# Attention on one Trainium2 core: joining the score products and the value products of two key chunks

## The chip, the cores and the metric

The kernel runs on one core of one Trainium2 chip. The metric is the device time of one execution in microseconds (us). The kernel before takes 992.52 us, the median of three runs (991.43 to 992.89).

## The reference

Attention with a sigmoid in place of the softmax, then a layer of eight experts with a skip gate, then a dense layer. The change lies in the attention alone.

```python
# q, k, v: (4, 12, 448, 64), float32
scale = 1.0 / np.sqrt(q.shape[-1])
scores = scale * np.matmul(q, k.transpose(0, 1, 3, 2)) - np.log(S)
attn = 1.0 / (1.0 + np.exp(-scores))
attn_out = np.matmul(attn, v)
x = attn_out.transpose(0, 2, 1, 3).reshape(B * S, H * D)      # 1792 x 768
...
# experts: tokens with x @ w_skip > 0 go through one of 8 experts and are added back
# dense layer: h = x @ w_in (768 -> 2048), elu(h) @ w_out (2048 -> 768)
```

## The kernel before, in words

The work has three stages, one after the other: attention (with the routing of the tokens behind it), experts, dense layer. In each of them the order of the instructions on TensorE, VectorE and ScalarE is the order in which the program is written (`manual_schedule`); the order on the DMA queues is set by a planner.

**Steps.** Attention runs over pairs of heads: 4 batches of 6 pairs are 24 steps, n = 0 to 23 (loop at line 448), and a 25th pass, n = 24, that only finishes the last pair. Two steps share a tile T of q and k (four heads); p is the step's place in its tile, hp its place in its batch. In a step the 448 keys are cut into four chunks of 112, c = 0 to 3 (line 479).

**One chunk.** `scores` (line 235) computes, for both heads of the pair, the transposed scores of one chunk: 112 keys by 448 queries. k is split into two float32r parts, kh and kl, and the parts of q lie stacked in qs, so that a head takes two MATMULs (line 239, out<-in `ps<-qs,kh` and `ps<-qs,kl`), four per chunk. Their output is a buffer `ps` of two PSUM banks; there are two such buffers in turn. ScalarE then takes the sigmoid of the whole buffer into the tile `at` (line 246). `mix` (line 250) multiplies a chunk of `at` by the values: for each head one float32 product with 64 output rows, the two heads side by side on the array (line 253, `po<-at,vt`). The trace shows a float32 product as two MATMULs, so a chunk has four of them, in two passes of two heads. The four chunks of a step accumulate in one PSUM bank `po`; behind the last of them VectorE copies it to `xT` (line 261).

**What follows what.** `at` has two buffers, so step n computes the scores of pair n and the value products of pair n - 1: the chunk loop issues scores of chunk c (pair n), then the value products of chunk c (pair n - 1).

**What else is in the chunk loop.** Behind chunks 1 and 3 come the splits of the next tile: ScalarE casts (line 227 for q, line 232 for k), VectorE subtracts (line 228 writes qs, line 233 writes kl). In the steps with p = 0 q is split, in those with p = 1 k. In nine steps a row tile of x is transposed by three plus three small MATMULs (line 138, `px`), copied out by VectorE behind chunk 1 and by ScalarE behind chunk 3 (line 283), and written to HBM. In the second step of batches 1 to 3 the gate logits of the batch before are computed behind chunk 0 (line 267) and copied by VectorE (line 275), and transposed behind chunk 2 (line 138, `pl`). Behind each chunk VectorE does up to two of the six operations that turn a float64 weight into float32 (`narrow`, lines 146 to 166; 18 weights in all, one per step at most, so six operations behind chunks 0, 1 and 2). In the last steps the routing of the first tokens is added (`soon`).

**After attention.** The last logits, the remaining row tiles and the routing follow; the routing yields the experts' numbers, by which the expert weights are fetched (line 693), and the tokens of each block (line 700).

The lines that matter here:

```python
for c in range(NCH):
    if n < steps:
        scores(at, c, p, *cur[1])
    if n:
        mix(c, n - 1, *prev, po)
    if nxt and n < steps and c % 2:
        (split_q, split_k)[p](c // 2, *nxt)
```

Of the kernel before, what the change touches and what calls it, by code (L numbers as in the profile page):

```python
# [32 lines left out]
E = 8  # L33
# [28 lines left out]


def _constants():
    """Identity, triangles and index ramps: they depend on shapes alone."""
    parts = {
        "ident": np.eye(P),
        "fold": np.arange(P)[:, None] % FEW == np.arange(P),
        "tri": np.triu(np.ones((P, P)), 1),
        "iota_r": np.tile(np.arange(P), (P, 1)),  # L70
        "iota_a": np.tile(np.arange(NHB) * P, (P, 1)),
        "rev": np.tile(E - np.arange(E), (P, 1)),
        "row": np.arange(P)[:, None],
        "ramp": np.tile(np.concatenate([np.arange(E), -np.arange(E)]), (P, 1)),
        "per_tok": GATE_UNIT / (np.arange(NTT)[None, :] * P + np.arange(P)[:, None] - NT),
        "tok": np.arange(NTT)[None, :] * P + np.arange(P)[:, None] - NT,
    }
    at = 0
    for name, a in parts.items():
        _CONST_COLS[name] = (at, a.shape[1])  # L80
        at += a.shape[1]
    return np.ascontiguousarray(np.concatenate(list(parts.values()), 1).astype(np.float32))
# [6 lines left out]
def build(nc, tc, a):  # L89
# [3 lines left out]
    with ExitStack() as top:  # L93
# [47 lines left out]
            nc.sync.dma_start(w, wide[i].rearrange("p (n t) -> p n t", t=2)[:, part])  # L141

        def narrow(dst, w, sg, mg, on_act):
            """Two words of a float64 to float32: sign, exponent - 896, top 23 bits."""
            lo, hi = w[:, :, 0], w[:, :, 1]
            nc.vector.tensor_scalar(sg, hi, NEG, None, op0=ALU.bitwise_and)
            yield
            if on_act:
                nc.scalar.activation(dst, hi.bitcast(F32), AF.Abs)
                nc.vector.tensor_scalar(dst, dst, LEAST, MOST, op0=ALU.max, op1=ALU.min)  # L150
            else:
                nc.vector.tensor_scalar(mg, hi, 2**31 - 1, None, op0=ALU.bitwise_and)
                yield
                nc.vector.tensor_scalar(
                    dst, mg.bitcast(F32), LEAST, MOST, op0=ALU.max, op1=ALU.min
                )
            yield
            nc.vector.scalar_tensor_tensor(
                sg, lo, 29, sg, op0=ALU.logical_shift_right, op1=ALU.bitwise_or
            )  # L160
            yield
            nc.vector.tensor_scalar(
                mg, dst.bitcast(I32), 4, NEG, op0=ALU.logical_shift_left, op1=ALU.bitwise_xor
            )
            yield
            nc.vector.scalar_tensor_tensor(
                dst.bitcast(I32), mg, 1, sg, op0=ALU.logical_shift_right, op1=ALU.bitwise_or
            )

# [1 line left out]
        ET = mybir.EngineType  # L171
        with ExitStack() as st:
            st.enter_context(tc.manual_schedule(engines={ET.PE, ET.Activation, ET.DVE}))
# [15 lines left out]
            nc.gpsimd.memset(zero_b, 0.0)  # L189

            def keep_warm(n):
                """Products of zeros that hold TensorE's clock up while it waits."""
                ps = pss.tile([P, 4, P], F32, name="idle", tag="ps")
                for _ in range(n):
                    nc.tensor.matmul(
                        ps, zero_b[:, 0], zero_b.to_broadcast([P, 4, P]), start=True, stop=True
                    )
# [124 lines left out]
            rt_tok = ert([NTT, P], "rt_tok", F16)  # L322

            def choices(a, z):
                """The experts of the tokens of tiles a to z; E stands for none."""
                w, sh = slice(a, z), [P, z - a, E]
                nc.gpsimd.tensor_scalar(oh1[:, w, E], lgt[:, w, E], 0.0, None, op0=ALU.is_le)
                nc.vector.reduce_max(mx[:, w, 0], lgt[:, w, :E], axis=AX.X)
                yield
                nc.vector.tensor_sub(dl[:, w], lgt[:, w, :E], mx[:, w].to_broadcast(sh))  # L330
                yield
                nc.vector.tensor_scalar(
                    skip[:, w], lgt[:, w, E], 0.0, float(NHB * P), op0=ALU.is_le, op1=ALU.mult
                )
                yield
                nc.vector.scalar_tensor_tensor(
                    sc[:, w], dl[:, w], 0.0, grid("rev", z - a, E), op0=ALU.is_ge, op1=ALU.mult
                )
                yield
                nc.vector.reduce_max(m2[:, w, 0], sc[:, w], axis=AX.X)  # L340
                yield
                nc.vector.tensor_add(m2[:, w, 0], m2[:, w, 0], skip[:, w])
                yield
                nc.vector.tensor_tensor(
                    oh[:, w], sc[:, w], m2[:, w].to_broadcast(sh), op=ALU.is_equal
                )
                yield
                with nc.allow_low_precision("whole numbers up to 14"):
                    nc.vector.reduce_sum(
                        per[a > 0][:, 0], oh1[:, w].rearrange("p t e -> p e t"), axis=AX.X  # L350
                    )
# [2 lines left out]
                run(choices(a, z))  # L354

            def positions(a, z, pool, tag):
                """How many tokens before each one have the same expert."""
                pos = pool.tile([P, z - a, E1], F32, name="pos", tag=tag)
                n, w = z - a, oh1[:, a:z]
                if a:  # L360
# [15 lines left out]
                return pos  # L376

            def places(a, z, pos):
                """The tokens' places in their half blocks."""
                w = slice(a, z)  # L380
                nc.vector.tensor_mul(t1[:, w], pos, oh1[:, w])
                yield
                nc.vector.reduce_sum(posv[:, w], t1[:, w], axis=AX.X)
                yield
                nc.vector.tensor_copy(pos_i[:, w], posv[:, w])
                yield
                nc.vector.tensor_scalar(sr_i[:, w, 0], pos_i[:, w], P - 1, None, op0=ALU.bitwise_and)
                yield
                nc.vector.tensor_copy(sr[:, w], sr_i[:, w])
                yield  # L390

            def spots(a, z):
                """One-hot rows of the tokens' places in their half blocks, times the tokens."""
                for t in range(a, z):
                    nc.vector.tensor_scalar(
                        rt_tok[:, t, :], iota_h, sr[:, t, :], con("tok")[:, t : t + 1],
                        op0=ALU.is_equal, op1=ALU.mult,
                    )
                    yield

            def sooner():
                """Routing of the first tiles."""
                yield from choices(0, SOON)
                for _ in range(NCH):
                    yield
# [42 lines left out]
            for n in range(steps + 1):  # L448
# [28 lines left out]
                    row = rows(done_rows, (nc.vector.tensor_copy, nc.scalar.copy))  # L477
                    done_rows += 1
                for c in range(NCH):
                    if n < steps:  # L480
                        scores(at, c, p, *cur[1])
                    if n:
                        mix(c, n - 1, *prev, po)
                    if nxt and n < steps and c % 2:
                        (split_q, split_k)[p](c // 2, *nxt)
                    if row is not None and c in (1, 3):
# [33 lines left out]
            for t in range(done_rows + 1, done_rows + 3):  # L520
                run(rows(t, tail_rows))

# [1 line left out]
            choose(SOON, NTT)  # L524
            cnt = ps1.tile([P, E], F32, name="cnt", tag="po")
            for k_, p in enumerate(per):
# [28 lines left out]
            nc.vector.reduce_sum(bs[:, 0, :], tmp, axis=AX.X)  # L555

            def halves():
                """One-hot columns of the tokens' half blocks."""
                fo = rt([NTT, E], "fo")
                nc.vector.tensor_mul(fo, bs.to_broadcast(sh), oh)  # L560
                yield
# [15 lines left out]
                    aa, sa.to_broadcast([P, NTT, NHB]), grid("iota_a", NTT, NHB), op=ALU.is_equal  # L577
                )

            # block b's expert, on partition b, and how many blocks there are  # L580
            own = rt([2, E], "own")
            nc.vector.tensor_add(span[:, 1], span[:, 0], nb[:, 0])
            nc.vector.scalar_tensor_tensor(
# [25 lines left out]
            nc.vector.tensor_scalar(used, inv, 0.0, None, op0=ALU.is_lt)  # L609
            nc.vector.tensor_copy(slot_off[:, :NHB], inv)  # L610

            # gates of the slots
            ex = rt([NTT, E], "ex")
            nc.scalar.activation(ex, dl, AF.Exp)
            sm = rt([NTT], "sm")
# [29 lines left out]
            nc.vector.tensor_copy(ct[:, 0], ordered)  # L645
            nc.vector.tensor_copy(tok[:, :, 0], con("tok")[:, :NOR])
            nc.vector.tensor_copy(iota_a[:, 0], con("iota_a")[:, :NOR])
# [1 line left out]
        kept = top.enter_context(ExitStack())  # L649
        with ExitStack() as st:  # L650
            st.enter_context(tc.manual_schedule(engines={ET.PE, ET.Activation, ET.DVE}))
# [113 lines left out]
                    )  # L765

            def product(o, h, n, a2, i, c, width, k0, total):
                """One chunk's part of a product whose stationary side is the tokens' columns."""
                t = slice(h * P, (h + 1) * P)
                for j in range(WCH // width):  # L770
                    w = slice(j * width, (j + 1) * width)
# [115 lines left out]
                        )  # L887

            def places_in_order():
                """Skipped tokens come first in the dense layer's order, then the blocks' tokens."""  # L890
                at = 0

                def part(*shape, dt=F32):
# [48 lines left out]
                    )  # L942

            def slot_order():
                """The dense layer's order, its first four columns behind the last block's."""
                og = acc_t[1][:, :NOR]
                for t in range(NOR):
                    nc.tensor.matmul(
# [13 lines left out]
                nc.vector.tensor_scalar_add(order, order_off, float(NT))  # L962

            def close(i):
                """With i blocks in all: the columns of the dense layer's first tokens."""
                if i == 0:
                    run(places_in_order())
                    order_rows()
# [45 lines left out]
            n = nc.values_load(n_blocks[:1, :1], min_val=0, max_val=NB)  # L1014
            level(0, n)

# [1 line left out]
        with ExitStack() as st:  # L1018
            st.enter_context(tc.manual_schedule(engines={ET.PE, ET.Activation, ET.DVE}))
            wsp = st.enter_context(tc.tile_pool(name="wsp", reuse_waits="tile", bufs=2))  # L1020
# [78 lines left out]
                return gh, gl  # L1099

            def regions(acc, t):
                """Where 128 tokens' 768 outputs lie: a bank, and half of one that two share."""
                yield acc[t], slice(0, 512), True
                half = acc[TB + t // 2]
                o = 256 * (t % 2)
# [137 lines left out]
```

## Time and profile before

| | |
|---|---|
| time, median of 3 runs (lowest, highest) | 992.52 us (991.43, 992.89) |
| span of the profiled execution, first to last instruction | 988.9 us |
| own time of the profiled execution | not recorded beside the span; the three runs lie 2.5 to 4.0 us above it |
| TensorE busy | 938.1 us, 95% of the span |
| VectorE, ScalarE busy | 590.0 us, 513.9 us |
| attention, first value product to last | 15.3 to 204.2 us |
| mean granted TensorE clock | 0.977 of full speed |

How to read it: a MATMUL's recorded end is modelled and matmuls overlap in the pipeline, so the busy share of TensorE tells little about how fast it goes. What counts is the distance from the start of one MATMUL to the start of the next. In the views below a row gives the start, the duration, engine, line, operation, the tensors (out<-in) and how many instructions were merged into it.

### The profile page before, as it was taken

The page shows a single profiled execution, that of the slowest core. Times are in us where ns is not written, and L with a number is a line of the kernel's source. Part 1 is how long each engine was busy: PE and PEld are TensorE (multiplying, and loading weights), DVE is VectorE, ACT ScalarE, POOL GpSimd, SP SyncE. Part 2 cuts the span into 40 slices and gives each one's busy share as a digit, 9 for nine tenths or more (in the row PEclk, how much of TensorE's full clock was granted, in tenths as well). Part 3 has the DMA queues.
Part 4 walks back from the last instruction along what each step waited for, and adds up shares of the span by engine and source line. Part 5 has one row for each costly group of instructions (what it writes and reads, how often), then busy time and mean ns, then how long its engine had stood idle before and what let it go on. Part 6 is the DMA issues. An engine that isn't in the chain of part 4 may idle for free. (4 is left out here: it accounts for less than half of the span.)

```text
span 988.9 us, 13865 instructions
## 1 busy us (share of the span) xinstructions
PE 938.1 (95%) x5310; PEld 745.3 (75%) x5310; DVE 590.0 (60%) x890; ACT 513.9 (52%) x700; POOL 60.2 (6%) x66
## 2 busy tenths in 40 slices
PE   8999999988896997978989999999999999999997
PEld 3444444448795897867879999988888888888997
DVE  4776777866743465448868888743444433443664
ACT  7767676634342543447745455444444434444664
POOL 0000000020111010011110000010000000000100
PEclk9999999998998999979999999999999999999999
DMA  9877877449955546558156334110001000000100
GB/s 247 264 228 233 278 219 236 163 166 379 410 185 189 183 158 254 180 205 316 47 210 227 97 96 120 57 65 1 17 17 32 29 37 1 1 1 1 65 1 33
DMA packets 33755, 139.56 MB, mean 141 GB/s; under 512 B 4634, under 2 KB 5274, under 8 KB 33650
## 3 DMA queue, kind: packets, MB, share of 16 engines
q1 hardware_dynamic: 29410, 119.17, 35.9%
q0 software_dynamic: 4240, 19.01, 5.3%
q8 instruction: 63, 1.03, 0.4%
q14 instruction: 42, 0.34, 0.1%
HBM read 117.58 MB, written 22.42 MB: 142 GB/s over the span
## 5 line engine op out<-in xcount | busy, mean ns | idle before, releaser
L719 DVE TENSOR_TENSOR wlo<-raw,whi 128x1536 fp32r<-128x1536 f32 x66 | 115.1, 1758 | 67.5 <-ACT whi L717 65.7
L246 ACT ACTIVATE at<-ps,bias 112x896 f32<-112x896 f32 x96 | 96.7, 1008 | 52.0 <-PE ps L239 50.1
L1094 DVE SCALAR_TENSOR_TENSOR m<-m,acc 128x512 f32<-128x512 f32 (+1 forms) x64 | 39.7, 621 | 140.6 <-ACT m L1093 140.6
L717 ACT CAST whi<-raw 128x1536 fp32r<-128x1536 f32 x66 | 96.5, 1478 | 52.1 <-PE acc L778 23.5
L1092 ACT ACTIVATE m<-acc 128x512 f32<-128x512 f32 (+1 forms) x64 | 34.9, 545 | 168.5 <-PE acc L1085 168.4
L1083 PE MATMUL acc<-x,wih 128*128 128x256 f32 (+1 forms) x360 | 121.5, 338 | 0.0
L1085 PE MATMUL acc<-x,wil 128*128 128x256 f32 (+1 forms) x360 | 121.5, 337 | 0.0
L1084 PE MATMUL acc<-x,wih 128*128 128x256 f32 (+1 forms) x360 | 121.3, 337 | 0.0
L1116 PE MATMUL acc<-wol,gh 128*128 128x256 f32 x320 | 101.1, 316 | 0.0
L1116 PE MATMUL acc<-woh,gl 128*128 128x256 f32 x320 | 100.6, 314 | 0.0
L1116 PE MATMUL acc<-woh,gh 128*128 128x256 f32 x320 | 100.4, 314 | 0.0
L253 PE MATMUL po<-at,vt 112*64 112x448 f32 x384 | 92.5, 563 | 0.0
L239 PE MATMUL ps<-qs,kh 128*112 128x448 f32 x192 | 79.5, 414 | 2.5 <-ACT kh L232 1.9
L239 PEld LDWEIGHTS ps<-qs,kh 128*112 128x112 f32 x192 | 33.9, 177 | 56.0 <-issue 39.5
L1073 DVE TENSOR_TENSOR wol<-wo,woh 128x768 fp32r<-128x768 f32 x64 | 61.2, 957 | 23.3 <-ACT woh L1072 22.9
L1085 PEld LDWEIGHTS acc<-x,wil 128*128 128x128 f32 x360 | 68.0, 189 | 7.7
L1083 PEld LDWEIGHTS acc<-x,wih 128*128 128x128 f32 x360 | 68.1, 189 | 6.4
L1084 PEld LDWEIGHTS acc<-x,wih 128*128 128x128 f32 x360 | 68.1, 189 | 6.3
L239 PE MATMUL ps<-qs,kl 128*112 128x448 f32 x192 | 71.5, 372 | 0.7 <-DVE kl L233 0.7
L1116 PEld LDWEIGHTS acc<-woh,gh 128*128 128x128 f32 x320 | 60.3, 189 | 10.1
L1116 PEld LDWEIGHTS acc<-wol,gh 128*128 128x128 f32 x320 | 60.3, 188 | 9.1
L1072 ACT CAST woh<-wo 128x768 fp32r<-128x768 f32 x64 | 53.3, 833 | 25.9 <-PE acc L1116 25.8
(236 smaller groups left out, 2036.1 us busy)
## 6 DMA issues: line engine op xcount, KB each, us to landing
raw<-in_w SPq DMA_DIRECT2D x66, 768.0 KB, 6.1
kr<-in_k SPq DMA_DIRECT2D x22, 448.0 KB, 6.3
raw<-in_wi SPq DMA_DIRECT2D x9, 768.0 KB, 7.8
raw<-in_wo SPq DMA_DIRECT2D x9, 768.0 KB, 7.2
vt<-in_v SPq DMA_DIRECT2D x12, 448.0 KB, 5.1
x_d<-xr SPq DMA_DIRECT2D x14, 384.0 KB, 2.7
raw<-in_wi SPq DMA_DIRECT2D x14, 384.0 KB, 3.0
raw<-in_wo SPq DMA_DIRECT2D x14, 384.0 KB, 3.0
```

Source lines behind the costliest of these rows:

```text
L239: nc.tensor.matmul(ps[:CP, j, :S], kk[:, 2 * p + j, c * CP : (c + 1) * CP], qs[:, p, j], start=(i == 0), stop=(i == 1),)
L246: nc.scalar.activation(at[:, :, c, :], ps[:CP, :, :S], AF.Sigmoid, bias=bias[:CP], scale=QK_SCALE)
L253: nc.tensor.matmul(po[64 * j : 64 * j + 64, :S], vt[:, 2 * (hp % 2) + j, c, :], at[:, j, c, :], start=(c == 0), stop=(c == NCH - 1),)
L717: nc.scalar.copy(w_hi, raw)
L719: nc.vector.tensor_sub(w_lo, raw, w_hi)
L1072: nc.scalar.copy(pair[0], wo_r[f])
L1073: nc.vector.tensor_sub(pair[1], wo_r[f], pair[0])
L1083: nc.tensor.matmul(o, a, b, start=(cc == 0), stop=False)
L1084: nc.tensor.matmul(o, a, c, start=False, stop=False)
L1085: nc.tensor.matmul(o, wil[:, cc], b, start=False, stop=(cc == KD - 1))
L1094: nc.vector.scalar_tensor_tensor(m[:, :n], m[:, :n], -1.0, ph[:, :n], op0=ALU.add, op1=ALU.max)
L1116: nc.tensor.matmul(o, a, b, start=(clears and f == 0 and k_ == 0), stop=(f == KF2 - 1 and k_ == 2), skip_group_check=True,)
```

## The change

The chunk loop issues the scores of two chunks, c and c + 1, and then the value products of the same two chunks of the preceding pair, each time c is even. At odd c it issues neither. Everything else in the loop stays where it was: splits, row tiles, logits, weight conversion and routing. The rest of the difference between the two files removes comments.

```diff
                 for c in range(NCH):
-                    if n < steps:
-                        scores(at, c, p, *cur[1])
-                    if n:
-                        mix(c, n - 1, *prev, po)
+                    if c % 2 == 0:
+                        for c2 in (c, c + 1):
+                            if n < steps:
+                                scores(at, c2, p, *cur[1])
+                        for c2 in (c, c + 1):
+                            if n:
+                                mix(c2, n - 1, *prev, po)
                     if nxt and n < steps and c % 2:
                         (split_q, split_k)[p](c // 2, *nxt)
```

TensorE, the first half of a step with neither logits nor a row tile (two chunks), before. `x2` stands for the two value products of a chunk:

```order
L239 MATMUL ps<-qs,kh 112x448
L239 MATMUL ps<-qs,kl 112x448
L239 MATMUL ps<-qs,kh 112x448
L239 MATMUL ps<-qs,kl 112x448
L253 MATMUL po<-at,vt 64x448 x2
L239 MATMUL ps<-qs,kh 112x448
L239 MATMUL ps<-qs,kl 112x448
L239 MATMUL ps<-qs,kh 112x448
L239 MATMUL ps<-qs,kl 112x448
L253 MATMUL po<-at,vt 64x448 x2
```

And now:

```order
L239 MATMUL ps<-qs,kh 112x448
L239 MATMUL ps<-qs,kl 112x448
L239 MATMUL ps<-qs,kh 112x448
L239 MATMUL ps<-qs,kl 112x448
L239 MATMUL ps<-qs,kh 112x448
L239 MATMUL ps<-qs,kl 112x448
L239 MATMUL ps<-qs,kh 112x448
L239 MATMUL ps<-qs,kl 112x448
L253 MATMUL po<-at,vt 64x448 x4
```

The same instructions stand in two runs in place of four, so TensorE goes from scores to value products and back once per two chunks in place of twice.

VectorE, one step (n = 8) from its conversion's first operation to the next step's, before (`sg`, `mg`, `mf` are the conversion, `qs` the split of q, `xr` a row tile, `xT` the copy of the finished pair):

```order
L146 TENSOR_SCALAR sg<-raw_106 128x768
L152 TENSOR_SCALAR mg<-raw_106 128x768
L228 TENSOR_TENSOR qs<-qr,qs 64x896
L283 COPY xr<-px 128x384
L154 TENSOR_SCALAR mf<-mg 128x768
L158 SCALAR_TENSOR_TENSOR sg<-raw_106,sg 128x768
L162 TENSOR_SCALAR mg<-mf 128x768
L166 SCALAR_TENSOR_TENSOR mf<-mg,sg 128x768
L261 COPY xT<-po 128x448
L228 TENSOR_TENSOR qs<-qr,qs 64x896
```

And now:

```order
L146 TENSOR_SCALAR sg<-raw_106 128x768
L152 TENSOR_SCALAR mg<-raw_106 128x768
L228 TENSOR_TENSOR qs<-qr,qs 64x896
L283 COPY xr<-px 128x384
L154 TENSOR_SCALAR mf<-mg 128x768
L158 SCALAR_TENSOR_TENSOR sg<-raw_106,sg 128x768
L261 COPY xT<-po 128x448
L162 TENSOR_SCALAR mg<-mf 128x768
L166 SCALAR_TENSOR_TENSOR mf<-mg,sg 128x768
L228 TENSOR_TENSOR qs<-qr,qs 64x896
```

The copy of `po`, which waits for the step's last value product, stands two conversion operations earlier. The order on ScalarE and on GpSimd is unchanged; on the SyncE queue single loads and stores trade places with their neighbours in three places.

## Rows read from the trace of the kernel before

**Rows 1.** The page, part 1: busy time, share and instructions of each engine.
```profile
PE 938.1 (95%) x5310; PEld 745.3 (75%) x5310; DVE 590.0 (60%) x890; ACT 513.9 (52%) x700; POOL 60.2 (6%) x66
```

**Rows 2.** Windows: us, busy of PE, PEld, DVE, ACT, POOL, PEclk, DMA share, GB/s.
```profile
14.00:50.00 36.00, 35.67 (x150) 15.50 (x152) 24.64 (x34) 28.59 (x32) 0.53 (x2) 1.00 0.93 268
50.00:100.00 50.00, 50.00 (x229) 22.09 (x227) 35.43 (x50) 36.45 (x40) 0.00 (x0) 1.00 0.76 235
...
175.00:200.00 25.00, 25.00 (x122) 11.65 (x120) 23.18 (x48) 15.95 (x18) 0.00 (x0) 1.00 0.47 161
```

**Rows 3.** Timeline of TensorE, one chunk in mid-stage and the start of the next.
```profile
69.76 0.46 PE L239 MATMUL ps<-qs,kh 128*112 128x448 f32 x1
70.06 0.36 PE L239 MATMUL ps<-qs,kl 128*112 128x448 f32 x1
70.26 0.36 PE L239 MATMUL ps<-qs,kh 128*112 128x448 f32 x1
70.46 0.37 PE L239 MATMUL ps<-qs,kl 128*112 128x448 f32 x1
70.75 0.97 PE L253 MATMUL po<-at,vt 112*64 112x448 f32 x4
71.66 0.46 PE L239 MATMUL ps<-qs,kh 128*112 128x448 f32 x1
```

**Rows 4.** Timeline of TensorE, the stage's last value products and the logits behind them.
```profile
200.22 3.98 PE L253 MATMUL po<-at,vt 112*64 112x448 f32 x20
204.13 1.73 PE L267 MATMUL lg<-xT,wgs 128*32 128x448 f32 x12
```

**Rows 5.** Timeline of TensorE in step 0, which has scores alone.
```profile
10.51 0.57 PE L239 MATMUL ps<-qs,kh 128*112 128x448 f32 x1
10.89 0.57 PE L239 MATMUL ps<-qs,kl 128*112 128x448 f32 x1
11.28 0.67 PE L239 MATMUL ps<-qs,kh 128*112 128x448 f32 x1
...
12.19 0.37 PE L239 MATMUL ps<-qs,kl 128*112 128x448 f32 x1
12.56 0.46 PE L239 MATMUL ps<-qs,kh 128*112 128x448 f32 x1
```

**Rows 6.** Timeline of ScalarE, the end of a step with a row tile.
```profile
76.87 1.01 ACT L246 ACTIVATE at<-ps,bias 112x896 f32<-112x896 f32 x1 [0.90 <-PE ps L239]
77.90 0.94 ACT L227 CAST qs<-qr 64x896 fp32r<-64x896 f32 x1
78.86 0.48 ACT L283 COPY xr<-px 128x384 f32<-128x384 f32 x1
79.37 1.01 ACT L246 ACTIVATE at<-ps,bias 112x896 f32<-112x896 f32 x1
```

**Rows 7.** Timeline of VectorE, from one step's first conversion operation to the next step's.
```profile
72.26 0.56 DVE L146 TENSOR_SCALAR sg<-raw 128x768 int32<-128x768 int32 x1
...
74.63 1.08 DVE L228 TENSOR_TENSOR qs<-qr,qs 64x896 fp32r<-64x896 f32 x1 [1.34 <-ACT qs L227]
...
77.55 0.55 DVE L162 TENSOR_SCALAR mg<-mf 128x768 int32<-128x768 int32 x1
78.14 0.96 DVE L166 SCALAR_TENSOR_TENSOR mf<-mg,sg 128x768 int32<-128x768 int32 x1
79.02 0.62 DVE L261 COPY xT<-po 128x448 f32<-128x448 f32 x1
...
80.78 0.56 DVE L146 TENSOR_SCALAR sg<-raw 128x768 int32<-128x768 int32 x1
```

**Rows 8.** Timelines of the SyncE queue and of GpSimd behind the routing: expert weights, tokens.
```profile
213.91 18.38 SPq L693 DMA_DIRECT2D raw<-in_w  x9
216.63 1.18 POOL L700 DMA_INDIRECT xg<-x_d,slot_tok  x1 [8.39 <-DVE val L622]
```

**Rows 9.** Groups by line, 0 to 205 us: busy, mean ns | idle before, releasers.
```profile
L239 PE MATMUL ps<-qs,kh 128*112 128x448 f32 x192 | 79.5, 414 | 2.5 <-ACT kh L232 1.9 <-ACT at L246 0.7
```

**Rows 10.** Cores: span and mean granted TensorE clock.
```profile
core 0: 988.9 us, clock 0.977
```

## The prediction
> **What bounds the kernel now.** I start from the page's busy times: TensorE is busy for 95% of the span, every other engine for 60% or less [rows 1]. The windows of the attention stage say the same more sharply: from 50 us on TensorE is busy without a gap at full granted clock, VectorE for some 70%, ScalarE for 73% [rows 2]. The groups by line add that TensorE waited for other engines for only 2.5 us in front of its 192 kh products, most of it in the first steps [rows 9]. So inside the stage TensorE's own sequence sets the pace, and only what changes the distance between its starts can change the time. Busy shares don't show that distance, because matmuls overlap; the timeline does.
>
> One chunk in mid-stage [rows 3]: kh starts at 69.76, then kl at 70.06 (0.30 later), kh at 70.26 and kl at 70.46 (0.20 each), the value products at 70.75 (0.29 later), the next chunk's kh at 71.66 (0.91 later). The period is 1.90 us. Inside a run of scores a start follows a start by 0.20; the first one and the way out take 0.30. So a run of scores pays about 0.10 to get in and 0.10 to get out.
>
> For the value products the end of the stage is the row to read: there 20 of them stand in one run, four of step 23's last chunk and 16 of step 24, from 200.22 to the logits at 204.13 [rows 4]. That is 3.91 us for five chunks, against 0.91 us for one chunk alone [rows 3]. A further chunk in the run therefore costs (3.91 - 0.91) / 4 = 0.75 us, not 0.91: each run pays 0.16 for its ends.
>
> **What the change is worth.** It moves no work between engines and adds or removes no instruction; it merges runs.
>
> - Scores: two runs of one chunk took 2 x 0.99 = 1.98 us. One run of two takes 0.99 + 4 x 0.20 = 1.79 us. Gain 0.19.
> - Value products: two runs took 2 x 0.91 = 1.82 us. One run of two takes 0.91 + 0.75 = 1.66 us. Gain 0.16; with the rounding of the rows, 0.15.
> - Together 0.34 us per pair of chunks: 3.80 before, 3.46 now.
> - Step 0 has only scores and step 24 only value products, and the change leaves their order as it is. In steps 1 to 23 there are two such pairs, 46 in all: 46 x 0.34 = 15.6 us. Where logits or row-tile transposes stand behind a pair, both runs are merged just the same.
>
> All of it lies on the path. Behind attention the kernel waits for results of attention: the first expert weights are fetched at 213.91 us, by expert numbers that the routing yields, and the tokens' gather waits 8.39 us for VectorE [rows 8]. So the rest of the kernel shifts as a block, and I cost it at nothing. The profiled execution has a span of 988.9 us and the median of the runs is 992.52, 3.6 above it. I take 15.6 from both: a span near 973, a time of **976.9 us**.
>
> One price in this sum is not shown: the step from the scores of one chunk to those of the next inside a run, where the buffer changes and ScalarE must have emptied the other one. I took 0.20, as between any two scores. In step 0 the same boundary stands. At half the clock it took 0.39 (10.89 to 11.28) against 0.38 for its neighbour, so the change of buffer by itself costs nothing that the rows resolve; once the clock was up it took 0.37 (12.19 to 12.56), because ScalarE had not emptied the buffer yet [rows 5]. The bounds are thus 0.20 and 0.37; nothing under 0.20 is to be had, since no start at full clock follows another of this size sooner. I take 0.20, since now two chunks of value products, 1.66 us, stand between one pair of scores and the next, and that is more than a sigmoid takes (1.01 us, rows 6).
>
> The Trainium skill prices a weight load by its columns over 1.2 GHz ("TensorE: Matmul & The Clock Gate", LDWEIGHTS). By that page alone, as an estimate, what a merge saves is one exposed load of 112 columns and one of 64, about 0.093 + 0.053 = 0.15 us, and the sum would be 46 x 0.15 = 6.7 us, 985.8 us. The rows above have both ends of each run in them and give more than twice that; they decide.
>
> **What is moved on the other engines.** ScalarE's order is unchanged. A sigmoid can start when its four score products are done; the two of a pair now become ready about 0.8 us apart in place of 1.9, so the second waits some 0.2 us for the first. Scores of the second chunk two pairs of buffers later start 3.46 us after those of its predecessor, so that 0.2 is hidden by more than 1 us.
>
> VectorE's copy of `po` into `xT` moves ahead of two conversion operations, 0.55 and 0.96 us long. Before, they ran first and the copy started at 79.02, when its product was long done [rows 7]. Now VectorE waits for the last value product of the step with 1.5 us of work queued behind it, and behind that stand the splits that the next tile needs. What hides this is VectorE's slack. From 72.26 to 80.78 a step with a conversion and a row tile took 8.52 us, 1.34 of them idle: 7.18 us of work [rows 7]. The step becomes 2 x 0.34 = 0.68 shorter, 7.84, so 0.66 of slack is left; a step without a row tile, shorter by the transposes, has less. The first split of k stands behind chunk 1 and is needed at the start of the next step, some 3.5 us later, so a lag of 1.5 us still does not reach TensorE. In the last 25 us VectorE is busy for 23.18 [rows 2]; should TensorE be held to VectorE's pace there, the gain of three or four steps, up to 4 x 0.68 = 2.7 us, is lost. On the SyncE queue three neighbours trade places, each a transfer that is used at least a step later: nothing.
>
> **Rivals.**
>
> - *ScalarE hands the buffers over late.* There are only two, and a pair fills both. If every second chunk paid 0.37 in place of 0.20, the loss is 46 x 0.17 = 7.8 us: 984.7 us. For it: step 0 shows that wait [rows 5], and with a cast and a row-tile copy ScalarE's chain for a pair is 1.03 + 0.96 + 0.51, and 1.01 for the other sigmoid, 3.51 us [rows 6], just over the new 3.46. Against: only nine steps have such a copy, one pair in each, and that pair is longer by its transposes; without the copy the chain is 3.00. 13 in 100. "TensorEngine Tiling" in the Trainium skill (PSUM Bottleneck) warns that emptying PSUM may become the limit once TensorE gets faster; by that rule this rival would be the likelier one, and the chain of 3.00 us in most pairs is what speaks against it here.
> - *VectorE becomes the bound.* If its slack were gone, the two conversion operations behind the waiting copy would lengthen every step: 23 x 1.5 = 34.5 us, less the 15.6 gained, +19 us: 1011 us. It decides once VectorE's work in a step exceeds the step. For it: the slack is small and the last stretch is nearly full [rows 2]. Against: the 7.18 us of work against 7.84 [rows 7], and half the stage with less work. 5 in 100.
> - *The gain is handed back.* Loads at 93% of DMA share from 14 to 50 us [rows 2] would hold the steps to the pace of the transfers, and the same for the weight conversion throughout: no change, 992.5 us. Only the first five steps run at that share, which is worth 5 x 0.68 = 3.4 us; against the rest speaks that later the share is 0.76 and 0.47. 5 in 100.
> - *More.* The mean granted clock of the span is 0.977 [rows 10], so some 2 x 0.023 x 988.9 = 45 us are spent at the lower of the two levels. If the shift of what follows attention moved one tenth of that up to the full level, 4.5 us of it would pass in half the time: 2.3 us more, 974.6 us; with the upper end of the gain per pair, 973. 5 in 100.
>
> The change does what it says: the order on TensorE shows the merged runs.
>
> **How the numbers follow.** The forecast, 974.5 to 980, has 72 in 100; its lower end is a gain of 0.39 per pair, its upper end the loss of the last steps' gain. With the case of more and the better part of the first rival, down to half its loss and a little beyond, the range is 973 to 984 us. What is left out is the worst of the first rival, the slow case and the handed-back one. A measurement tells 0.2%, 2 us, from no change: faster by more than that takes the forecast, the first rival and the last, 0.90; within it the handed-back case, 0.05; slower the VectorE case, 0.05.
>
> **What would show it.** Right: value products in rows of eight starting about 1.66 us before the next kh; kh after kl 0.20 apart across the chunk boundary; the two-chunk period 3.46; the last value products' run starting near 185 in place of 200 us; the first weight fetch near 198. Wrong: idle time in front of `ps` ended by ScalarE's sigmoid, or in front of kh and kl ended by the splits; a two-chunk period above 3.6; the fetch shifted by less than 12 us.

## The result, and the profile after

The changed kernel takes 979.07 us, the median of four runs (977.41 to 980.67), against 992.43 us for the kernel before (four runs): a ratio of 0.9865, with a 95% interval of 0.9846 to 0.9885. The profiled execution took 977.41 us, with a span of 975.6 us against 988.9.

The page, part 1, of the changed kernel (columns as in [rows 1]):

```profile
PE 925.7 (95%) x5310; PEld 755.5 (77%) x5310; DVE 589.7 (60%) x890; ACT 509.4 (52%) x700; POOL 60.2 (6%) x66
```

The same instructions, TensorE as busy a share as before: the busy share tells nothing of the gain. The windows of the attention stage (columns as in [rows 2]):

```profile
14.00:50.00 36.00, 34.48 (x158) 17.79 (x158) 25.44 (x34) 29.14 (x33) 1.03 (x2) 1.00 0.92 266
50.00:100.00 50.00, 50.00 (x249) 26.33 (x246) 39.85 (x58) 38.53 (x44) 0.00 (x0) 1.00 0.84 252
100.00:150.00 50.00, 49.79 (x250) 26.64 (x249) 39.72 (x57) 37.90 (x44) 0.00 (x0) 1.00 0.90 277
```

Between 50 and 100 us TensorE issues 249 matmuls where it issued 229 [rows 2]; VectorE's busy time rises from 35 to 40 us in 50, the DMA share from 0.76 to 0.84. And TensorE now stands idle for 1.5 us between 14 and 50 us, where it was 0.3 us [rows 2], and for 0.2 us between 100 and 150 us.

Two joined chunks on the timeline of TensorE, to be read against [rows 3]:

```profile
101.47 1.72 PE L253 MATMUL po<-at,vt 112*64 112x448 f32 x8
103.12 0.45 PE L239 MATMUL ps<-qs,kh 128*112 128x448 f32 x1
103.41 0.37 PE L239 MATMUL ps<-qs,kl 128*112 128x448 f32 x1
103.62 0.37 PE L239 MATMUL ps<-qs,kh 128*112 128x448 f32 x1
103.82 0.36 PE L239 MATMUL ps<-qs,kl 128*112 128x448 f32 x1
104.02 0.36 PE L239 MATMUL ps<-qs,kh 128*112 128x448 f32 x1
...
104.63 0.37 PE L239 MATMUL ps<-qs,kl 128*112 128x448 f32 x1
104.93 1.72 PE L253 MATMUL po<-at,vt 112*64 112x448 f32 x8
```

Two chunks of value products take 103.12 - 101.47 = 1.65 us, two chunks of scores 104.93 - 103.12 = 1.81 us, together 3.46. The start of the second chunk's kh, 104.02, follows the kl at 103.82 by 0.20: here the buffer changes at no cost.

The end of the stage on the timelines of TensorE and of the SyncE queue, to be read against [rows 4] and [rows 8]:

```profile
186.01 4.73 PE L253 MATMUL po<-at,vt 112*64 112x448 f32 x24
190.68 2.28 PE L267 MATMUL lg<-xT,wgs 128*32 128x448 f32 x12
```

```profile
200.99 11.25 SPq L696 DMA_DIRECT2D raw<-in_w  x3
```

The last logits start 13.45 us earlier (204.13 to 190.68), the first expert weights are fetched 12.92 us earlier (213.91 to 200.99), and the span ends 13.3 us earlier. So the gain is made in attention, and the rest follows it. It is 2 to 3 us short of the 15.6 that the joined runs are worth. The waits of 14 to 190 us show where some of that went (who waited for whom: us in total, times, longest):

```profile
PEld ps L239 <- ACT at L246: 15.0, 22, 0.7
...
PEld ps L239 <- DVE kl L233: 2.1, 2, 1.6
PE ps L239 <- DVE kl L233: 1.5, 2, 1.3
```

The first row looks like a new wait for ScalarE and is none. It is the idle time of the weight load at each change from value products to scores, which was put down to "issue" before. The distance between the starts shows it: from the last pass of value products to the next kh it is 0.47 us in both kernels, and the 1.65 us above leave no room for a wait beside the 1.66 that the rows of the kernel before gave. The rows that count are those for kl: two waits of TensorE, in which it stands still:

```profile
35.52 0.45 PE L239 MATMUL ps<-qs,kh 128*112 128x448 f32 x1
37.30 0.46 PE L239 MATMUL ps<-qs,kl 128*112 128x448 f32 x1 [1.33 <-DVE kl L233]
...
142.19 0.45 PE L239 MATMUL ps<-qs,kh 128*112 128x448 f32 x1
142.86 0.46 PE L239 MATMUL ps<-qs,kl 128*112 128x448 f32 x1 [0.21 <-DVE kl L233]
```

kl follows kh after 1.78 and 0.67 us in place of 0.30. VectorE's timeline says why kl came late, in both places:

```profile
35.22 0.56 DVE L146 TENSOR_SCALAR sg<-raw 128x768 int32<-128x768 int32 x1 [3.31 <-DMA raw<-in_wo]
...
36.16 1.08 DVE L233 TENSOR_TENSOR kl<-kr,kh 128x896 fp32r<-128x896 f32 x1
...
140.73 0.60 DVE L146 TENSOR_SCALAR sg<-raw 128x768 int32<-128x768 int32 x1 [3.04 <-DMA raw<-in_wi]
```

The conversion's first operation, which stands behind chunk 0, waited 3.3 and 3.0 us for its float64 weight; the split that yields kl stands behind it. On the SyncE queue that weight had been issued behind the loads of k:

```profile
23.44 1.11 SPq L217 DMA_DIRECT2D kr<-in_k  x2
24.61 0.58 SPq L141 DMA_DIRECT2D raw<-in_wo  x1
...
130.08 1.14 SPq L217 DMA_DIRECT2D kr<-in_k  x2
131.27 0.58 SPq L141 DMA_DIRECT2D raw<-in_wi  x1
```

From issue to first use went 10.6 and 9.5 us. The first of these waits was there before the change: VectorE waited 3.10 us and TensorE's kl came 0.2 late. A faster TensorE made more of it.

A third, smaller loss lies in step 1, the first with joined chunks. There the second chunk's kh follows the kl before it by 0.56 us in place of 0.20, because ScalarE had not yet emptied the buffer:

```profile
15.01 0.37 PE L239 MATMUL ps<-qs,kl 128*112 128x448 f32 x1
15.57 0.46 PE L239 MATMUL ps<-qs,kh 128*112 128x448 f32 x1 [0.19 <-ACT at L246]
```

A fourth is in the last logits: their twelve products took 2.28 us in place of 1.73.

The reading to test, called theory A in what follows: each joined pair gives 0.34 us, and some 2 us are given back where a split of k stands behind a conversion whose weight is late. Theory B: VectorE's copy of `po`, which now waits ahead of two conversion operations, costs the missing time. Theory C: ScalarE, with two score buffers, sets the pace of the changed kernel.

### The profile page after: what moved, and what is told of

Its sections match the earlier page's. It is cut to its first block, busy times and chain, and to the rows that moved or that the text cites. A ratio compares the mean times of both kernels' runs of the same rounds, so it can differ in the third digit from the quotient of the medians.

```text
span 975.6 us, 13863 instructions
## 1 busy us (share of the span) xinstructions
PE 925.7 (95%) x5310; PEld 755.5 (77%) x5310; DVE 589.7 (60%) x890; ACT 509.4 (52%) x700; POOL 60.2 (6%) x66
## 5 line engine op out<-in xcount | busy, mean ns | idle before, releaser
L246 ACT ACTIVATE at<-ps,bias 112x896 f32<-112x896 f32 x96 | 91.7, 1004 | 41.1 <-PE ps L239 41.0
L253 PE MATMUL po<-at,vt 112*64 112x448 f32 x384 | 82.3, 551 | 0.0
L239 PE MATMUL ps<-qs,kh 128*112 128x448 f32 x192 | 76.2, 397 | 2.6 <-ACT kh L232 2.4
L1101 DVE TENSOR_TENSOR gl<-m,gh 128x512 fp32r<-128x512 f32 (+1 forms) x64 | 40.0, 625 | 40.5 <-ACT gh L1100 40.5
```

The source lines that it names most:

```text
L239: nc.tensor.matmul(ps[:CP, j, :S], kk[:, 2 * p + j, c * CP : (c + 1) * CP], qs[:, p, j], start=(i == 0), stop=(i == 1),)
L246: nc.scalar.activation(at[:, :, c, :], ps[:CP, :, :S], AF.Sigmoid, bias=bias[:CP], scale=QK_SCALE)
L253: nc.tensor.matmul(po[64 * j : 64 * j + 64, :S], vt[:, 2 * (hp % 2) + j, c, :], at[:, j, c, :], start=(c == 0), stop=(c == NCH - 1),)
L1101: nc.vector.tensor_sub(gl[:, :n], m[:, :n], gh[:, :n])
```

## The experiments

The runs' times scatter by several us, more than the waits in question. So each profile is also read at two places: the start of the last logits (the end of attention), and the stretch from the first scores of step 1, the first step that the change touches, to there. The kernel before: 14.29 to 204.13, 189.84 us. The changed kernel: 14.31 to 190.68, 176.37 us, 13.47 less.

That stretch is not free of the clock either. In three of the traces (the split ahead of the conversion, the copy put back, the changed kernel again) TensorE is still at the lower level when step 1 begins: the mean granted clock between 14 and 17 us is 0.57 to 0.61 there, against 0.97 in the changed kernel's first trace. From the first scores of step 1 to its first value product it takes 2.51 to 2.66 us in these three and 2.26 in the other, so 0.25 to 0.40 us of their stretch is the clock's.

### Half of the joins

```diff
+group = {0: (0, 1), 1: (), 2: (2,), 3: (3,)}[c]
-if c % 2 == 0:
-    for c2 in (c, c + 1):
+for c2 in group:
```

> Only chunks 0 and 1 of a step are joined; chunks 2 and 3 stand as before the change. Theory A (each joined pair gives 0.34 us, read from the starts; some 2 us are lost again where a split of k stands behind a weight conversion whose weight has not arrived): 23 pairs x 0.34 = 7.8 us, less about 1 us of such waits, so 985 to 986 us, and the last logits near 197 us in the trace. Theory B (VectorE's copy, now ahead of two conversion operations, costs the missing 2 us): the copy stands where it stood before, so the full 7.8 us, 984.5 us. Theory C (ScalarE's two buffers set the pace of the changed kernel): half the joins already reach that pace, near 980 us.

Measured: 984.49 us, ratio 0.9924 (0.9901 to 0.9948) to the kernel before, 992.04 in this comparison. From step 1 to the last logits 14.91 to 198.21, 183.30 us: 6.54 less than before. The wait for kl of this trace is in its waits (1.4 us for the load, 1.2 for the matmul, one place), and 7.8 less some 1.1 us more of such waiting than before is the 6.5. Half the joins bring half the gain; that speaks against theory C, by which they would have brought most of it. The time alone can't tell theory A from theory B: it lies at the 984.5 of B, and below the 985 to 986 of A. What speaks against B is the wait for kl, which is there although the copy stands where it stood before.

### The split ahead of the conversion

```diff
-if conv is not None and next(conv, 1):
+if conv is not None and c >= (p if nxt else 0) and next(conv, 1):
```

> The changed kernel, but in the steps that split k the conversion's operations start behind chunk 1's split (chunks 1 to 3 in place of 0 to 2). Theory A: the two waits of TensorE for kl (1.5 us at 35 us and 0.45 us at 142 us) go, the last logits start near 189 us in place of 190.7, and the time falls by 1.7 us to about 977.3. Theory B: more conversion work than now stands behind the copy, so the waits stay or grow, 979 to 981. Theory C: no change, 979.

Measured: 978.70 us, ratio 0.9866 (0.9837 to 0.9895). Both waits for kl are gone from the waits, as theory A has it, and still attention ends at 190.92. Here is where the time went, on the timelines of VectorE and of TensorE:

```profile
143.39 0.56 DVE L146 TENSOR_SCALAR sg<-raw 128x768 int32<-128x768 int32 x1 [4.27 <-DMA raw<-in_wi]
...
149.84 0.56 DVE L146 TENSOR_SCALAR sg<-raw 128x768 int32<-128x768 int32 x1 [1.07 <-DMA raw<-in_wo]
```

```profile
151.48 1.69 PE L267 MATMUL lg<-xT,wgs 128*32 128x448 f32 x10
154.05 0.94 PE L267 MATMUL lg<-xT,wgs 128*32 128x448 f32 x2 [0.88 <-DVE xT L261]
```

The late weight now holds VectorE behind the split. The next weight is late as well, by 1.07 us, and holds the operations and the copy of `po` that stand behind it; the logits wait for that copy's `xT`, with a gap of some 1.7 us. The wait was moved, not removed: what stood behind the late weight has changed, the late weight has not. A further 0.4 us of this stretch is the lower clock at its start. The expected 1.7 us did not come.

### The copy put back

```diff
-if c == NCH - 1:
-    nc.vector.tensor_copy(xT[:, hp, b * S : (b + 1) * S], po[:, :S])
+if n and c == NCH - 1:
+    b1, hp1 = divmod(n - 1, NP)
+    nc.vector.tensor_copy(xT[:, hp1, b1 * S : (b1 + 1) * S], po[:, :S])
```

The first pair of lines goes from `mix`, the second stands in the chunk loop behind the products.

> The changed kernel with VectorE's copy of po put back behind chunk 2's conversion operations, so that VectorE's order is that of the kernel before and only TensorE's runs are joined. Theory A: both waits for kl stay, time 979 plus or minus 0.5, last logits near 190.7 us. Theory B: the waits go, 977. Theory C: 979.

Measured: 977.91 us, ratio 0.9864 (0.9832 to 0.9896). VectorE's order is that of the kernel before, and both waits for kl are still there, a little longer:

```profile
PEld ps L239 <- DVE kl L233: 2.9, 2, 1.7
PE ps L239 <- DVE kl L233: 2.4, 2, 1.4
```

From step 1 to the end of attention 14.75 to 192.19, 177.44 us, 1.07 more than in the changed kernel: 0.25 of it is the lower clock at the start of step 1, the rest the longer waits. A second profile of the changed kernel, further down, comes to 177.24 us with the same clock there. So the copy's place is not the cause of the waits for kl.

In the last logits theory B does hold. VectorE at the end of attention, in the changed kernel and then in this one (where the copy is line 487 and the routing's rows are line 393), and this one's logits:

```profile
187.78 0.62 DVE L261 COPY xT<-po 128x448 f32<-128x448 f32 x1 [0.83 <-PE po L253]
...
188.77 0.55 DVE L162 TENSOR_SCALAR mg<-mf 128x768 int32<-128x768 int32 x1
189.35 0.96 DVE L166 SCALAR_TENSOR_TENSOR mf<-mg,sg 128x768 int32<-128x768 int32 x1
190.23 1.20 DVE L395 TENSOR_SCALAR rt_tok<-iota_h,sr,early_cst 128x128 f16<-128x128 f16 x5
191.35 0.61 DVE L261 COPY xT<-po 128x448 f32<-128x448 f32 x1
```

```profile
189.84 1.20 DVE L393 TENSOR_SCALAR rt_tok<-iota_h,sr,early_cst 128x128 f16<-128x128 f16 x5
192.30 0.62 DVE L487 COPY xT<-po 128x448 f32<-128x448 f32 x1 [1.27 <-PE po L253]
```

```profile
192.19 1.74 PE L265 MATMUL lg<-xT,wgs 128*32 128x448 f32 x12
```

In the changed kernel two conversion operations stand behind the waiting copy, and the last copy starts 0.67 us after the logits. With the copy put back they are done before it; VectorE is then 1.27 us early for the last copy, and the twelve logits take 1.74 us as before the change. That part of the missing time, some 0.55 us, is the copy's place. The median lies 1.2 us under that of the changed kernel, although its stretch is longer, which shows how little a time alone says here.

### The second weight loaded early

```diff
 wide_load(wides[0], 0)
+wide_load(wides[1], 1)
...
-if narrowed + 1 < 2 * FA:
+if 0 < narrowed < 2 * FA - 1:
```

> The changed kernel with the second weight's load issued before the steps, next to the first one's, in place of behind the loads of k in step 2. Theory A: the wait of 1.5 us at 35 us goes, since the weight is there; the one at 142 us stays; last logits near 189.4 us, time about 977.8. If the transfer is late because the queues are full, not because it is issued late, the wait comes back elsewhere (first k or v of the second tile) and the time stays at 979. Theories B and C: 979.

Measured: 978.10 us, ratio 0.9858 (0.9825 to 0.9891). The timeline of TensorE at the first place:

```profile
35.57 0.46 PE L239 MATMUL ps<-qs,kh 128*112 128x448 f32 x1
35.87 0.36 PE L239 MATMUL ps<-qs,kl 128*112 128x448 f32 x1
```

kl follows kh after 0.30 us: the wait is gone. So is the one at 142 us, which I expected to stay. The edit also changed the order of the SyncE queue later on, and the weight that was late there is now issued ahead of the loads of k:

```profile
124.93 0.33 SPq L141 DMA_DIRECT2D raw<-in_wi  x1
...
128.54 1.26 SPq L217 DMA_DIRECT2D kr<-in_k  x2
```

From step 1 to the end of attention: 14.31 to 188.66, 174.35 us, 15.49 less than before the change, against 15.6 forecast. Neither VectorE's nor TensorE's order differs from the changed kernel's; what differs is the SyncE queue, where these two weights are issued earlier and some loads and stores beside them trade places. VectorE's waits for weights between 14 and 190 us fall from 7.4 us to 0.5. That shows the cause of the two waits.

The time does not show it: from the first fetch to the end of the span this profile took 977.2 - 199.00 = 778.2 us, the changed kernel's 975.6 - 200.99 = 774.6, of a part that is the same in both.

### The changed kernel again, and the version that the runs point to

The next three ran beside one another, on a chip where the kernel before took 988.64 us (12 runs, 987.27 to 990.84).

> The changed kernel once more, beside the next two on the same chip. All theories: 978 to 979 us; last logits 190.7 plus or minus 0.7 us, with the same waits for kl near 35 and 142 us. It shows how far two profiles of one program differ ahead of the expert weights' fetch and behind it.

Measured: 979.39 us, six runs from 975.91 to 984.38, ratio 0.9921 (0.9897 to 0.9944). The two waits for kl are there again, 2.1 us in all in place of 1.5; from step 1 to the end of attention it took 14.82 to 192.06, 177.24 us. The last logits start 1.4 us later than in the first profile, more than the 0.7 allowed for: step 1 begins 0.5 us later, the lower clock there costs 0.3, the longer waits 0.6.

The version adds to the early load that the routing's rows of the 25th pass (`rt_tok`) no longer stand ahead of VectorE's last copy:

```diff
-if n > SOON_STEP:
+if SOON_STEP < n < steps:
...
-if n > SOON_STEP + 2:
+if SOON_STEP + 2 < n < steps:
...
-run(soon)
 logits(B - 1)
+run(soon)
```

In the changed kernel those rows and the two conversion operations ahead of them made the last copy late, and the last two of twelve logits products waited for it; this is why the twelve took 2.28 us against 1.73 before. Either remedy takes the wait away: the copy put back did it with the rows in place, this version does it with the conversion in place.

> The early load of the fourth run, and in the 25th pass the routing's one-hot rows no longer ahead of VectorE's last copy of po; they follow the last logits. Theory A: no wait for kl at all, the last logits start near 188.7 us and their run of twelve takes 1.7 us in place of 2.3; the fetch of the expert weights starts near 198.4 us, 2.5 earlier than in the changed kernel; time about 976.5. Theories B and C: the fetch stays near 200.9 and the time at 979.

Measured: 975.89 us (973.71 to 978.44), ratio 0.9877 (0.9859 to 0.9895) to the kernel before and, by medians, 3.5 us under the changed kernel of the same comparison, though the runs of the two overlap. Timelines of VectorE, TensorE and the SyncE queue:

```profile
188.75 0.62 DVE L261 COPY xT<-po 128x448 f32<-128x448 f32 x1
```

```profile
188.63 1.74 PE L267 MATMUL lg<-xT,wgs 128*32 128x448 f32 x12
```

```profile
198.41 14.12 SPq L697 DMA_DIRECT2D raw<-in_w  x6
```

No wait for kl, twelve logits in 1.74 us, the fetch at 198.41: 15.50 us earlier than in the kernel before, where 15.6 had been forecast. These are the numbers that theory A gave.

### Runs of four chunks

```diff
-if c % 2 == 0:
-    for c2 in (c, c + 1):
-        if n < steps:
-            scores(at, c2, p, *cur[1])
-    for c2 in (c, c + 1):
-        if n:
-            mix(c2, n - 1, *prev, po)
+if n < steps and c % 2 == 0:
+    for c2 in (c, c + 1):
+        scores(at, c2, p, *cur[1])
+if n and c == 0:
+    for c2 in range(NCH):
+        mix(c2, n - 1, *prev, po)
```

> Scores of chunks 2 and 3 and of chunks 0 and 1 of the next step stand in one run of four, and the value products of all four chunks in another: one change of kind per step less than in the changed kernel. It leaves TensorE nothing between the pairs of scores, so the third and fourth chunk of a run must wait until ScalarE has emptied the two buffers. Theory A (the hand-over is hidden in the changed kernel by 1.65 us of value products, not free): 0.34 us saved and some 0.7 to 0.8 waited for ScalarE per step, 23 steps, so about 9 us slower than the changed kernel, 986 to 990. If the hand-over were free: 979 - 23 x 0.34 = 971. Theory C (ScalarE already sets the pace in the changed kernel): the run of four changes nothing, 979.

Measured: 982.69 us, ratio 0.9943 (0.9922 to 0.9963): 3.3 us above the changed kernel of the same comparison. Less than the 7 or more that I expected, but with the sign of theory A. A run of four on the timeline of TensorE:

```profile
104.70 0.37 PE L239 MATMUL ps<-qs,kl 128*112 128x448 f32 x1
105.34 0.46 PE L239 MATMUL ps<-qs,kh 128*112 128x448 f32 x1 [0.28 <-ACT at L246]
...
106.24 0.46 PE L239 MATMUL ps<-qs,kh 128*112 128x448 f32 x1
106.54 0.36 PE L239 MATMUL ps<-qs,kl 128*112 128x448 f32 x1
```

The third chunk's kh follows after 0.64 in place of 0.20, and it and the fourth pay their way in again (0.30 from kh to kl). That is 0.44 + 0.09 + 0.10 and more than the 0.34 of the change of kind that is saved, so some 0.29 us lost each time. A boundary of 0.64 to 0.66 us stands in only ten places of this trace; in the other steps transposes stand between the chunks and hide most of the wait. Ten times 0.29 is 2.9 of the 3.3 us by which the stretch from step 1 to the last logits is longer than the changed kernel's (179.69 against 176.37). So two score buffers don't bear four chunks in a run, and the value products between the pairs are what hides ScalarE in the changed kernel.

## Why the prediction was right

Its main step was the price of a joined pair, 0.34 us, read from three rows of the kernel before: scores at 0.99 + 4 x 0.20, value products at 0.91 + 0.75. Measured: 1.81 and 1.65, together 3.46 us, as forecast. That the gain comes from the joins is shown by half of them, which bring half. Right too was the price taken for the boundary inside a run of scores: 0.20 us, the lower of its two bounds. The upper bound of 0.37 was not the worst: where nothing stands between the pairs, in the run of four, the boundary takes 0.64.

That the rest shifts as a block held within half a us in this pair of profiles: the fetch came 12.92 us earlier, the end 13.3. That is in part luck: the length of that rest differs by up to 6.5 us between profiles (see the last section), and the 2 us between the 976.9 forecast and the 979.07 measured lie inside that spread. The stretch in the trace is the closer test.

In the trace, what is missing of the 15.6 us comes mainly from the step on the other engines, and one of the prediction's own signs of being wrong did appear: idle time in front of kl ended by the splits, 1.5 us. It said that a lag of VectorE of 1.5 us does not reach TensorE, and counted VectorE's work; it did not count that VectorE itself waits. In the last logits the lag of the copy does reach TensorE, for 0.55 us. The weights for the conversion were late already (VectorE waited 3.10 us at 35 us before the change), and I read the DMA share only as a rival in which the whole gain is handed back. By the rows of the changed kernel, TensorE lost 1.48 us and 0.37 us in the two places beyond the normal 0.30 (0.2 of it was lost before as well), some 0.45 in step 1, where the second chunk's buffer was not yet empty, and 0.55 in the last logits: together 2.7 us of 15.6, which leaves the 12.9 by which the fetch moved. The version with the early load and the cleared tail has three of these four back and shows 15.5; the fourth, in step 1, is partly balanced by the 0.2 to 0.3 us that the kernel before had itself lost to a late kl.

The first rival, a late hand-over by ScalarE at 0.37 a pair, holds only in step 1. The second, VectorE as the bound of every step, does not hold: with the copy put back the waits for kl stayed. What it names, operations queued behind the waiting copy, costs 0.55 us at the end of attention and nothing that these rows show in the steps. The Trainium skill's "TensorEngine Tiling" (PSUM Bottleneck) says that emptying PSUM may become the limit; it says so of a fourfold speed-up by tiling, and here a pair went from 3.80 to 3.46 us. In this case emptying is not the limit for pairs, while in runs of four TensorE waits for the sigmoid in ten places. The estimate by the price that the Trainium skill's "TensorE: Matmul & The Clock Gate" (LDWEIGHTS) gives for the two loads, 6.7 us, is refuted by the 13.4 measured: a change of kind costs more than that. The trace's own rows of the two loads are longer, 0.17 and 0.14 us; what else a change of kind is made of, no run here separates.

## What to carry to other kernels

Where matmuls of two kinds alternate, measure from start to start what each kind costs alone and in a run; the difference, times the number of runs that can be joined, is what an order gives, and a run must end before the buffers that its results fill run out. Before counting such a gain, look through the other engines' waits for one that is hidden just barely: a faster TensorE uncovers it. Here a transfer that was late was cured by issuing it earlier; putting something else behind it only moved the wait.

## What the runs showed of the hardware that was not expected

The part behind the first fetch of expert weights is the same code in all kernels, and its length in the profiles differs by 6.5 us: 775.0 before, 774.6 after, 771.7 for the changed kernel again, 772.8 with the copy put back, 778.2 with the early load, 773.7 for the last version (span less start of the fetch). The granted clock explains part of this at most. The cores' views of the early load, of the last version and of the copy put back, span and mean clock:

```profile
core 0: 977.2 us, clock 0.974
```

```profile
core 0: 972.1 us, clock 0.978
```

```profile
core 0: 974.7 us, clock 0.974
```

Of the two levels, 1.2 and 2.4 GHz, the first spent 2 x 0.026 x 977.2 = 51 us at the lower one, the second 43; 8 us more at half speed cost up to 4 us, and their last parts differ by 4.5. But the copy put back has the same mean clock as the early load, 0.974, and a last part 5.4 us shorter, so something else differs too, and what it is stays open. In the start of the kernel the lower level lasted until 11.8 us in one profile and until about 16 in others (starts of scores 0.37 apart in place of 0.20), though TensorE's order up to step 1 is the same. A gain of 2 us in this kernel can be seen in a stretch of the trace, hardly in a time.
